# An attention and gated-convolution kernel on one core: sums over 576 columns, 66 weight columns, a 64-row mask, another order of TensorE's runs and shifted due times

## The chip, the cores and the metric

The program runs on one core of one Trainium2 chip. The metric is device time in microseconds of one execution. Five engines take part, each with an instruction queue of its own: TensorE (PE, the matmuls; PEld is its weight load), VectorE (DVE), ScalarE (ACT), GpSimd (POOL) and SyncE (SP), which issues all transfers.

## What is computed

```python
# q, k, v: (8, 8, 576, 64); s: (8, 8, 576)
scores = q @ k.T / sqrt(64)
cum = cumsum(maximum(s, 0))
scores = where(causal, -1e9, scores + minimum(cum_k - cum_q, 0))
attn = exp(scores - max(scores)); attn = attn / (sum(attn) + 1e-9)
x = (attn @ v) as (8, 576, 512)
h = maximum(x @ w_in, 0)                       # w_in: 512 x 1024
conv = three taps along the sequence, one weight per channel
out = (h * sigmoid(conv)) @ w_out              # w_out: 1024 x 512
```

## The kernel before

**Pairs.** The 64 heads (8 batches of 8) are worked in 32 pairs; one head of a pair lies in partitions 0 to 63, the other in 64 to 127, so TensorE works both at once in tiles of 64 rows. The sequence of 576 is cut into tiles of 128 (the last has 64). Only the half of the scores that the causal mask keeps is computed: 576, 448, 320, 192 and 64 columns for the five key tiles. A pair has these tasks, named by a prefix and the pair's number:

- `sh` (L803): a first score pass that gives each row's maximum, in four parts of two matmul steps; `mx` (L820, L825): the maxima on VectorE; `tn`, `rt`, `ds`: they are turned, copied and sent into tile `eq`.
- `sc` (L884): the scores proper, keys on partitions, in four parts (288; 288; 448 and 64; 320 and 192 columns) of four steps each, two PSUM banks a part; `ex` (L906): the exponential on ScalarE into `pt`; `mk` (L919): the triangular part is cleared on GpSimd.
- `ad` (L962): the exponentials of tiles 1 (its last 320 columns) to 4 are added into tile `ad`, three additions a head, on VectorE or GpSimd.
- `sum` (L997): column sums by matmul with a one-hot weight, in tiles of 32 weight columns; `pv` (L944): the values, also in 32-column tiles; `gd`, `inv`, `ri`, `rb`, `nm`: the inverse of the sum is spread over the partitions by way of DRAM, and the values are multiplied by it; `xh`, `xl` split the result in two parts for the next stage.
- `hi` (L756) and `lo` (L760) split queries and keys in two parts before the pair's scores; `dr` (L770) loads the rows of the bias into `ek`.

The second stage works a batch, once its four pairs are done, in two halves: `h` (L1094, 8 blocks of 12 matmuls), ScalarE and VectorE work on each, `ul` (L1161) on GpSimd, then `o` (L1189, 4 blocks of 24 matmuls), `oe` and `st`.

**Early and late pairs.** For pairs before `B0 = 9` the causal mask is added to the scores on TensorE by matmuls of `mask` and `unit` with all 128 rows (L888), there is no `ad`, and the sums go over all 1600 columns. From pair 9 on, `mk` and `ad` are used and TensorE's work is bound in groups: group n holds the `sh` of pair n+1, the `sc` of pair n and the `sum` and `pv` of pair n-1, in the order of the table `ORDER`, and nothing else runs on TensorE in between. The first of a group waits for all that its members need.

```python
ORDER = ("sh0", "sh1", "sh2", "sum", "pv", "sc0", "sh3", "sc1", "sc2", "sc3")
```

**The order of the rest.** A planner (`Sched.play`) runs the task graph once with estimated durations and gives each engine, whenever it is free, the ready task with the smallest due time (`tag`). The order that comes out is the program order of each engine's queue; on the chip only semaphores hold it. The planner also picks PSUM banks and buffers, lets an addition go to VectorE or GpSimd, and does not let operations that are marked as needing both engines' shared way to memory run on both at once.

Of the kernel before, what the change touches and what calls it, by code (L numbers as in the profile page):

```python
# [59 lines left out]
ORDER = ("sh0", "sh1", "sh2", "sum", "pv", "sc0", "sh3", "sc1", "sc2", "sc3")  # L60

# [240 lines left out]
def kernel(  # L302
# [44 lines left out]
    unit = const.tile([P, P], BF16, name="unit")  # L347
# [3 lines left out]
    junk = const.tile([P, S], BF16, name="junk")  # L351
# [16 lines left out]
    ad_t = const.tile([P, 2, W_T[2]], F32, name="ad")  # L368
# [3 lines left out]
    ri_t = const.tile([P, RS], F32, name="ri")  # L372
# [88 lines left out]
    def c_ident(e):  # L461
        make_identity(nc, ident)
        nc.gpsimd.tensor_copy(unit, ident)
# [258 lines left out]
    direct = []  # L722
    last_ek, last_v, last_nm = [None], [None], []
# [8 lines left out]
    def c_rt(n):  # L732

        return n * 0.461e-3

    def pair(p):
# [30 lines left out]
        def d_rows(e):  # L767
# [9 lines left out]
            [last_ek[0], *t_pads[: p + 1]] + (t_bx if 2 * p < DIRECT else [t_rows_d]), a_sh - DRA, d_rows,  # L777
# [9 lines left out]
        for i, part in enumerate(SH_PARTS):  # L787
            pbs = [psb(), psb()]

            def sh_mm(e, part=part, pbs=pbs):  # L790
                o = 0
                for tau, c0, c1 in part:
                    dst = [bank(pb, o, o + c1 - c0) for pb in pbs]
                    qs = slice(P * tau, P * tau + P)
                    for k in range(2):
                        for j, r in enumerate(lanes):
# [10 lines left out]
            t_mm = add(f"sh{p}.{i}", [("PE", 2 * c_rt(w))], [t_hi, t_dr, t_eb],  # L807
# [4 lines left out]
            for j in range(2):  # L812
                o = 0
                for tau, c0, c1 in part:
                    def sh_max(e, j=j, tau=tau, c0=c0, c1=c1, o=o, pb=pbs[j]):
# [17 lines left out]
                        add(f"mx{p}.{j}.{tau}.{c0}", [("DVE", (0.15 if tau == L and c0 == 0 else 0.22) + (c1 - c0) / 0.96e3)],  # L833
# [31 lines left out]
        for i, part in enumerate(SC_PARTS):  # L865
            pbs = [psb(), psb()]

            def sc_mm(e, part=part, pbs=pbs):
                o = 0
                for t, c0, c1 in part:  # L870
                    i0, cn = P * t + c0, c1 - c0
                    ks = slice(P * t, P * t + P)
                    dst = [bank(pb, o, o + cn) for pb in pbs]
                    st = S_t[sb.slot].rearrange("p a c -> p (a c)")
                    for k in range(4):
                        for j, r in enumerate(lanes):
                            if k < 3:
                                kk, kq = ((2, 3), (0, 3), (2, 1))[k]
                                l = st[r, kk * S + P * t : kk * S + P * t + P]
                                m = st[r, kq * S + i0 : kq * S + i0 + cn]  # L880
                            else:
                                l = EK_t[ek.slot][r, ks]
# [417 lines left out]
```

## Time and profile before

| what | value |
|---|---|
| device time, three runs | 810.75, 812.44 and 814.55 us (median 812.44) |
| span of the profiled execution, first to last instruction | 810.0 us |
| TensorE busy | 772.9 us (95%) |
| VectorE busy | 596.5 us (74%) |
| ScalarE busy | 442.1 us (55%) |
| GpSimd busy | 311.6 us (38%) |
| chain that ended last, TensorE's share | 87% |

The device time of the profiled execution itself is not listed apart from its span; the timed runs lie 0.75 to 4.55 us above the span. A busy share is a mean over stages that have different limits; matmuls overlap, so a busy TensorE need not be one at its peak. What a change is worth is read in the stage where it acts.

### The profile page before, as it was taken

How to read it: one execution, taken by the hardware profiler on the slowest of the kernel's cores; microseconds unless marked ns; L12 is line 12 of the kernel's file. 1: busy time of each engine (PE TensorE's matmuls, PEld its weight loads, DVE VectorE, ACT ScalarE, POOL GpSimd, SP SyncE). 2: the span in 40 equal slices, each digit the busy share in tenths (PEclk: the TensorE clock that was granted, in tenths of full speed). 3: DMA queues.
4: the chain of work that ended last, by engine and by line, in shares of the span. 5: the costliest groups of instructions: out<-in, count | busy, mean ns of one | idle time of the engine just before them, and what ended most of it. 6: DMA issues, size and time to landing. Idle time of an engine off the chain costs nothing.

```text
span 810.0 us, 21043 instructions
## 1 busy us (share of the span) xinstructions
PE 772.9 (95%) x8371; PEld 693.5 (86%) x8371; DVE 596.5 (74%) x1379; ACT 442.1 (55%) x982; POOL 311.6 (38%) x411
## 2 busy tenths in 40 slices
PE   2699998989999999999999999999999999999998
PEld 2576777779998999999998999999998999998997
DVE  8779778885577778777778778777777778734632
ACT  4364565637455645646555645646455645645633
POOL 7054452433334443443434443543434433422212
PEclk9999999999999999999999999999999999999999
DMA  7355433320213222122213222132213211111001
GB/s 221 122 161 153 134 100 95 120 89 19 82 46 87 77 82 75 46 90 74 82 45 91 73 82 75 46 92 72 83 45 92 72 54 44 44 42 41 16 23 37
DMA packets 49805, 63.24 MB, mean 78 GB/s; under 512 B 5679, under 2 KB 38767, under 8 KB 49647
## 3 DMA queue, kind: packets, MB, share of 16 engines
q1 hardware_dynamic: 49707, 61.91, 25.1%
q8 instruction: 65, 1.06, 0.5%
q14 instruction: 33, 0.27, 0.1%
HBM read 48.60 MB, written 13.04 MB: 76 GB/s over the span
## 4 chain that ended last, share of the span: by engine, by line
PE 87%; DVE 4%; ACT 2%; POOL 2%; DMA 2%; issue 2%; SPq 0%; ACTq 0%; DVEq 0%; POOLq 0%
PE ps L1189 25%; PE ps L1094 25%; PE ps L884 15%; PE pv L944 10%; PE ps L803 6%; PE ps L997 5%; ACT pt L906 1%; DMA ek<-bx 1%; DVE junk L825 1%; DVE ct L1131 1%; PE ps L888 1%; DMA rb<-ri_d 1%; DVE ct L612 0%; ACT s L756 0%; DVE ct L1119 0%
## 5 line engine op out<-in xcount | busy, mean ns | idle before, releaser
L1189 PE MATMUL ps<-u,wo 128*128 128x288 f32 x1536 | 218.0, 299 | 2.0 <-POOL u L1161 1.4
L1161 POOL TENSOR_TENSOR u<-ct,u 128x576 fp32r<-128x576 f32 x64 | 96.7, 1510 | 314.2 <-ACT u L1157 286.2
L1094 PE MATMUL ps<-x,wi 128*128 128x290 f32 x1536 | 215.9, 298 | 0.0
L1189 PEld LDWEIGHTS ps<-u,wo 128*128 128x128 f32 x1536 | 207.6, 188 | 4.7 <-POOL u L1161 1.9
L1094 PEld LDWEIGHTS ps<-x,wi 128*128 128x128 f32 x1536 | 209.1, 190 | 1.1
L906 ACT ACTIVATE pt<-ps,bias_sb 128x288 f32<-128x288 f32 (+4 forms) x384 | 153.5, 477 | 64.7 <-PE ps L884 64.3
L1131 DVE SCALAR_TENSOR_TENSOR ct<-ht,cw_sb,ct 128x288 f32<-128x288 f32 (+1 forms) x256 | 134.3, 525 | 71.7 <-ACT ct L1117 66.8
L825 DVE CUSTOM_DVE_ANT_0 junk<-ps,mask 128x448 bf16<-128x448 f32 (+3 forms) x256 | 108.3, 423 | 27.7 <-PE ps L803 3.5
L884 PE MATMUL ps<-s 64*128 64x288 f32 (+4 forms) x1152 | 125.1, 314 | 3.3 <-DVE r L825 2.5
L884 PEld LDWEIGHTS ps<-s 64*128 64x128 f32 x1152 | 101.7, 189 | 13.0 <-ACT pt L906 5.7
L1105 ACT ACTIVATE ht<-ps 128x289 f32<-128x289 f32 x128 | 52.7, 412 | 83.6 <-PE ps L1094 82.1
L944 PE MATMUL pv<-pt,v 128*32 128x448 f32 (+4 forms) x1536 | 96.0, 395 | 0.0
L919 POOL TENSOR_SCALAR_AFFINE_SELECT pt<-pt 128x128 f32<-128x128 f32 x230 | 67.3, 312 | 73.2 <-ACT pt L906 70.8
L760 POOL TENSOR_TENSOR s<-raw,s 128x1152 fp32r<-128x1152 f32 x31 | 86.5, 2790 | 15.3 <-ACT s L756 9.6
L944 PEld LDWEIGHTS pv<-pt,v 128*32 128x32 f32 x1536 | 54.9, 111 | 38.0 <-issue 29.8
L884 PE MATMUL ps<-eq,ek 64*128 64x288 f32 (+4 forms) x384 | 74.4, 325 | 0.0
L803 PE MATMUL ps<-s 64*128 64x288 f32 (+4 forms) x384 | 66.5, 331 | 6.0 <-DVE r L820 3.2
L1117 ACT ACTIVATE ct<-ht,cw_sb 128x288 f32<-128x288 f32 x126 | 67.7, 537 | 5.8
L1206 ACT COPY ob<-ps 128x288 f32<-128x288 f32 x63 | 25.0, 397 | 80.5 <-PE ps L1189 68.1
L1150 DVE TENSOR_TENSOR ct<-ct,ht 128x576 f32<-128x576 f32 x64 | 54.4, 851 | 16.7 <-ACT ct L1144 16.7
L803 PE MATMUL ps<-ek,eb 64*128 64x288 f32 (+4 forms) x384 | 58.2, 320 | 6.4 <-DMA ek<-bx 6.4
L1144 ACT ACTIVATE ct<-ct 128x576 f32<-128x576 f32 x64 | 43.6, 681 | 31.5 <-DVE ct L1131 31.2
(87 smaller groups left out, 802.8 us busy)
## 6 DMA issues: line engine op xcount, KB each, us to landing
raw<-qk SPq DMA_DIRECT2D x32, 576.0 KB
v<-vp SPq DMA_DIRECT2D x32, 320.0 KB
rb<-ri_d SPq DMA_DIRECT2D x64, 144.0 KB
outT<-ob SPq DMA_DIRECT2D x64, 144.0 KB
ht<-w_out SPq DMA_DIRECT2D x16, 256.0 KB
w<-w_in SPq DMA_DIRECT2D x8, 512.0 KB
ri_d<-ri SPq DMA_DIRECT2D x32, 72.0 KB
rows_d<-bx SPq DMA_DIRECT2D x1, 1215.0 KB
```

Of the source, the lines that this page charges most:

```text
L760: tt_on(e)(st[:, 0:2, :], R_t[raw.slot], st[:, 2:4, :].bitcast(F32), op=ALU.subtract)
L803: nc.tensor.matmul(dst[j], l, m, start=(k == 0), stop=(k == 1))
L825: nc.vector.tensor_tensor_reduce(out=junk[:, 0 : c1 - c0], in0=bank(pb, o, o + c1 - c0), in1=mask[:, S - w + c0 : S - w + c1], scale=1.0, ...
L884: nc.tensor.matmul(dst[j], l, m, start=(k == 0), stop=(k == 3))
L906: nc.scalar.activation(PT_t[pts[j].slot][0:jt, O_T[t] + c0 : O_T[t] + c1], bank(pb, o, o + c1 - c0)[0:jt], AF.Sigmoid, bias=bias_sb[0:jt, ...
L919: nc.gpsimd.affine_select(out=reg, in_=reg, pattern=[[1, dg]], compare_op=ALU.is_ge, fill=0.0, base=0, channel_multiplier=-1,)
L944: nc.tensor.matmul(pvt[gs, o0 : o0 + c1 - c0], vt[0:jt, t, gs], PT_t[pts[g // 2].slot][0:jt, O_T[t] + c0 : O_T[t] + c1], start=(t == 0), s ...
L1094: nc.tensor.matmul(bank(hb, 0, XW), l, r, start=(k == 0), stop=(k == len(seq) - 1))
L1117: nc.scalar.activation(o, src, AF.Copy, scale=w)
L1131: nc.vector.scalar_tensor_tensor(cc[:, lo:hi], h_[:, sh + lo : sh + hi], cw_sb[:, 3 * f + k : 3 * f + k + 1], cc[:, lo:hi], op0=ALU.mult, ...
L1161: tt_on(e)(uu[:, 1], C_t[ct.slot], uu[:, 0].bitcast(F32), op=ALU.subtract)
L1189: nc.tensor.matmul(bank(pb, 0, HS), l, r, start=(fp == 0 and k == 0), stop=(fp == NF // 2 - 1 and k == len(seq) - 1),)
```

## The change

There are seven parts.

1. `ORDER` is now sums, values, then score parts and maxima parts in turn.
2. For late pairs `ad` has a fourth addition, over 448 columns, so that it covers tiles 0 (from column 128) to 4. The sums then go over 128 columns of `pt` and 448 of `ad`: 576 a head in place of 1024. One head is finished before the other.
3. The score matmuls of the last key tile load 66 weight columns in place of 128.
4. The early mask is built on 64 rows (`mrow`, which lies in the memory of `ad`, and `unit` of 64 columns) and is added in steps of 64 columns, inside the 64-row tiles. It is also added in `sh`, so that the early maxima are plain reductions. Late additions wait for the last use of `mrow`.
5. The planner's price of score and maxima parts has a floor for narrow matmuls.
6. A table `DUE` shifts the due time of nearly every task by its own number; the code that adds it stands at the end.
7. `ri` is no tile of its own any more (the reciprocal is made in place), `junk` is smaller, and the second `dr` no longer waits for the first.

```diff
-ORDER = ("sh0", "sh1", "sh2", "sum", "pv", "sc0", "sh3", "sc1", "sc2", "sc3")
+ORDER = ("sum", "pv", "sc0", "sh0", "sc1", "sh1", "sc2", "sh2", "sc3", "sh3")
...
+DUE = {
...
+        "0 10.83 1 6.21 2 3.03 3 -14.83 4 -47.29 5 82.43 6 30.85 7 -2.83 8 5.75 9 -54.34 "
...
+        nc.gpsimd.memset(mrow, 0.0)
+        for j in range(2):
+            for i in range(2):
+                h = mrow[D * j : D * j + D, 0, i]
+                nc.gpsimd.affine_select(
...
-            [last_ek[0], *t_pads[: p + 1]] + (t_bx if 2 * p < DIRECT else [t_rows_d]), a_sh - DRA, d_rows,
+            [last_ek[0] if p > 1 else None, *t_pads[: p + 1]] + (t_bx if 2 * p < DIRECT else [t_rows_d]), a_sh - DRA, d_rows,
...
+                        if k and p < B0 and tau < L:
+                            for i_ in range(0 if tau else 1, 2):
+                                for j, r in enumerate(lanes):
+                                    d0 = c1 - c0 - D * (2 - i_)
+                                    nc.tensor.matmul(
+                                        dst[j][:, d0 : d0 + D], mrow[r, 1, i_], unit[r],
+                                        start=False, stop=False,
+                                    )
...
-                        if tau == L and c0 == 0:
+                        if plain(tau, c0):
...
+                    kn = min(P, J_T[t] + 2)
+                    dst = [bank(pb, o, o + cn)[0:kn] for pb in pbs]
...
-                                l = st[r, kk * S + P * t : kk * S + P * t + P]
+                                l = st[r, kk * S + P * t : kk * S + P * t + kn]
...
-                            for j in range(2):
-                                nc.tensor.matmul(
-                                    dst[j][:, 0:dg], mask[:, S - P : S], unit[:, 0:dg],
-                                    start=False, stop=False,
-                                )
+                            for i_ in range(dg // D):
+                                for j, r in enumerate(lanes):
+                                    nc.tensor.matmul(
+                                        dst[j][:, D * i_ : D * i_ + D], mrow[r, 0, i_, 0:kn], unit[r],
+                                        start=False, stop=False,
+                                    )
...
-                for t in range(2, NT):
+                for t in range(1, NT):
...
-                        (0, pt[:, 0:S]), (P, pt[:, O_T[1] : O_T[1] + P]), (2 * P, ad_t[:, j, :])
+                        (0, pt[:, 0:P]), (P, ad_t[:, j, :])
...
-            nc.vector.reciprocal(ri_t, rs_t)
+            nc.vector.reciprocal(rs_t, rs_t)
...
+    for t in sch.tasks:
+        t.tag += shift.get(due(t.name), 0.0)
```

How many matmuls of `h` and `o` stand between two groups also changes: between the sums of pairs 9 to 31 there were 60, 72, 120 or 132 of them, and now there are 48 in nine of the places, 72 in two, and 96 to 168 elsewhere.

TensorE at the sums of a late pair, before (`pt_92`, `pt_93`: the two heads' exponentials; the first row is the end of the maxima part `sh2`, the last one the start of the values):

```order
L803 MATMUL ps_70<-ek_84,eb 128x64
L997 MATMUL ps_65<-pt_92,onehot 32x144 x4
L997 MATMUL ps_65<-pt_93,onehot 32x144 x4
L997 MATMUL ps_65<-pt_92,onehot 32x16
L997 MATMUL ps_65<-pt_92,onehot 32x112
L997 MATMUL ps_65<-pt_93,onehot 32x16
L997 MATMUL ps_65<-pt_93,onehot 32x112
L997 MATMUL ps_65<-ad,onehot 32x32
L997 MATMUL ps_65<-ad,onehot 32x144 x2
L944 MATMUL pv<-pt_92,v_91 32x128 x2
```

The same place now, where L1328 is `o` and L1136 and L1082 are the sums and values:

```order
L1328 MATMUL ps_65<-u_1188,wo 128x288 x6
L1136 MATMUL ps_66<-pt_92,onehot 32x128
L1136 MATMUL ps_66<-ad,onehot 32x16
L1136 MATMUL ps_66<-ad,onehot 32x144 x3
L1136 MATMUL ps_66<-pt_93,onehot 32x128
L1136 MATMUL ps_66<-ad,onehot 32x16
L1136 MATMUL ps_66<-ad,onehot 32x144 x3
L1082 MATMUL pv<-pt_92,v_90 32x128 x2
```

The sums have 10 matmuls in place of 18 and follow the `o` matmuls directly; the maxima parts have moved behind the score parts.

GpSimd between two groups that stand close together, before (L919 is `mk`, L962 `ad`, L760 `lo` of the next pair, L1161 `ul`; the first row is the fifth clearing of this pair):

```order
L919 AFFINE_SELECT pt_93<-pt_93 128x128
L919 AFFINE_SELECT pt_93<-pt_93 64x64
L919 AFFINE_SELECT pt_92<-pt_92 128x128 x2
L919 AFFINE_SELECT pt_93<-pt_93 128x128 x2
L962 TENSOR_TENSOR ad<-ad,pt_92 128x192
L962 TENSOR_TENSOR ad<-pt_93 128x320
L760 TENSOR_TENSOR s_83<-raw_81,s_83 128x1152
L1161 TENSOR_TENSOR u_977<-ct_107,u_977 128x576
```

And now, with 48 matmuls between the groups (L1057 is `mk`, L1099 `ad`, L883 `lo`):

```order
L1057 AFFINE_SELECT pt_93<-pt_93 128x128
L1057 AFFINE_SELECT pt_93<-pt_93 64x64
L1099 TENSOR_TENSOR ad<-pt_92 128x448
L1057 AFFINE_SELECT pt_92<-pt_92 128x128
L1099 TENSOR_TENSOR ad<-pt_93 128x448
L1057 AFFINE_SELECT pt_92<-pt_92 128x128
L1057 AFFINE_SELECT pt_93<-pt_93 128x128 x2
L883 TENSOR_TENSOR s_82<-raw_80,s_82 128x1152
```

Both wide additions stand between the clearings, and the other six go to VectorE. In all, 42 of the 46 wide additions are GpSimd's.

SyncE at the start, before (`ek_84` and `ek_85` belong to pairs 0 and 1):

```order
L770 DMA ek_84<-bx 9x1x576 x2
L544 DMA rows_d<-bx 60x5184
L744 DMA raw_81<-qk 128x1152
L770 DMA ek_85<-bx 9x1x576 x2
L770 DMA ek_86<-rows_d 9x576 x2
```

And now:

```order
L893 DMA ek_84<-bx 9x1x576 x2
L893 DMA ek_85<-bx 9x1x576 x2
L665 DMA rows_d<-bx 60x5184
L867 DMA raw_81<-qk 128x1152
L893 DMA ek_86<-rows_d 9x576 x2
```

The load for pair 1 has moved ahead of the store of `rows_d` and of the load of `raw_81`.

## Rows read from the trace of the kernel before

**Rows 1.** The page: its first line.

```profile
span 810.0 us, 21043 instructions
```

**Rows 2.** Busy time in stretches: from, to, length; PE, PEld, DVE, ACT, POOL; clock; DMA.

```profile
41.00:211.00 170.00, 160.51 (x1859) 130.51 (x1860) 134.28 (x334) 94.72 (x222) 69.23 (x47) 0.97 0.36 108
211.00:702.00 491.00, 490.47 (x5511) 450.09 (x5513) 382.39 (x882) 277.10 (x623) 202.34 (x303) 1.00 0.23 70
```

**Rows 3.** Timeline of PE, one group: start us, length us, line, operation, shape, count.

```profile
347.56 0.40 PE L803 MATMUL ps<-s 64*128 64x288 f32 x2
347.79 0.30 PE L803 MATMUL ps<-ek,eb 64*128 64x288 f32 x2
347.92 0.30 PE L803 MATMUL ps<-s 64*128 64x288 f32 x2
...
348.65 0.28 PE L803 MATMUL ps<-ek,eb 64*128 64x64 f32 x2
348.86 0.79 PE L997 MATMUL ps<-pt,onehot 128*32 128x144 f32 x22
...
349.82 0.30 PE L944 MATMUL pv<-pt,v 128*32 128x128 f32 x1
...
352.67 0.68 PE L884 MATMUL ps<-s 64*128 64x288 f32 x6
...
355.43 0.44 PE L884 MATMUL ps<-s 64*128 64x64 f32 x5
...
355.93 0.68 PE L884 MATMUL ps<-s 64*128 64x320 f32 x5
...
357.12 1.06 PE L1189 MATMUL ps<-u,wo 128*128 128x288 f32 x6
```

**Rows 4.** Timeline of PE at two changes of tile shape.

```profile
347.33 0.29 PE L1189 MATMUL ps<-u,wo 128*128 128x288 f32 x1
...
711.09 0.29 PE L1189 MATMUL ps<-u,wo 128*128 128x288 f32 x1
711.31 0.33 PE L997 MATMUL ps<-pt,onehot 128*32 128x144 f32 x4
```

**Rows 5.** Chain that ended last: start, length, line, count.

```profile
368.74 1.60 PE ps L1189 x12
```

**Rows 6.** Weight loads by form: count, busy us, mean ns of one, idle before.

```profile
L884 PEld LDWEIGHTS ps<-s 64*128 64x128 f32 x1152 | 101.7, 189 | 13.0 <-ACT pt L906 5.7 <-DVE r L825 3.6 <-issue 0.5
L944 PEld LDWEIGHTS pv<-pt,v 128*32 128x32 f32 x1536 | 54.9, 111 | 38.0 <-issue 29.8
```

**Rows 7.** Timeline of ACT, the same group.

```profile
353.56 0.89 ACT L906 ACTIVATE pt<-ps,bias_sb 128x288 f32<-128x288 f32 x2 [1.73 <-PE ps L884]
...
356.08 2.99 ACT L906 ACTIVATE pt<-ps,bias_sb 128x448 f32<-128x448 f32 x8 [0.37 <-PE ps L884]
```

**Rows 8.** Tile `ad`: additions on VectorE (ns min/median/max), on GpSimd (busy us, mean ns).

```profile
L962 DVE TENSOR_TENSOR ad<-ad,pt x69: 210/346/2877, 224.0 to 724.3; 128x64 f32<-128x64 f32 x46, 128x192 f32<-128x192 f32 x23
...
L962 POOL TENSOR_TENSOR ad<-pt 128x320 f32<-128x320 f32 x5 | 4.4, 888 | 0.0
```

**Rows 9.** Timeline of GpSimd: one `lo`.

```profile
342.66 2.89 POOL L760 TENSOR_TENSOR s<-raw,s 128x1152 fp32r<-128x1152 f32 x1 [0.46 <-ACT s L756]
```

**Rows 10.** Timelines of SyncE, GpSimd and TensorE at the start.

```profile
14.19 0.48 SPq L544 DMA_DIRECT2D rows_d<-bx  x1
...
16.48 4.22 SPq L770 DMA_DIRECT2D ek<-bx  x2
...
11.95 1.40 POOL L486 MEMSET ek<- 10x576 f32 x2
...
24.58 0.75 PE L803 MATMUL ps<-ek,eb 64*128 64x288 f32 x2 [5.11 <-DMA ek<-bx]
```

**Rows 11.** Maxima on VectorE by form, 20 to 210 us.

```profile
L825 DVE CUSTOM_DVE_ANT_0 junk<-ps,mask 128x448 bf16<-128x448 f32 x19 | 11.8, 622 | 3.5 <-PE ps L803 1.3 <-DVE r L825 0.7 <-ACT wo L688 0.2
L825 DVE DVE_READ_ACCUMULATOR2_ANT r<- 128x1 f32 x96 | 8.0, 83 | 0.0
```

More of the change, by code (lines that the diff above doesn't have):

```diff
@@ L59, with due @@
 B0 = 9
-ORDER = ("sh0", "sh1", "sh2", "sum", "pv", "sc0", "sh3", "sc1", "sc2", "sc3")
+ORDER = ("sum", "pv", "sc0", "sh0", "sc1", "sh1", "sc2", "sh2", "sc3", "sh3")
+KINDS = {
+    "sh": ("mx",), "tn": ("rt", "ds"), "sc": ("ex", "mk", "ad"), "pv": ("sum",),
+    "nm": ("gd", "inv", "ri", "rb", "xh", "xl"), "g": ("re", "ce", "ta", "ga", "mu", "uh", "ul"),
+    "o": ("oe", "st"),
+}
+DUE = {
+    "x":
+        "s -33.34 masks -20.61 ident 7.58 eb -10.97 cum 15.92 rows_d -2.56 bias_cp 15.79 cw 4.06 "
+        "cwq 18.7 cwh 29.2",
+    "pads":
+        "0 4.99 1 20.21 2 -5.6",
+    "ind":
[78 rows of a table added]
+}
+def due(name):
+    kind, rest = re.match(r"([a-z]+)(.*)", name).groups()
+    if not rest or kind in ("bias", "rows"):
+        return "x:" + name
+    for of, kinds in KINDS.items():
+        if kind in kinds:
+            kind = of
+    n = 2 if kind in ("h", "g", "o", "wo") else 1
+    return kind + ":" + ".".join(re.findall(r"^[\d.]*", rest)[0].split(".")[:n])
 class Buf:
@@ L350 @@
     cw_sb = const.tile([P, NF * 3], F32, name="cw_sb")
-    junk = const.tile([P, S], BF16, name="junk")
+    junk = const.tile([P, W_T[1]], BF16, name="junk")
     wi = const.tile([P, 2, NC, DF], F32R, name="wi")
@@ L366 @@
     rb_t = const.tile([P, S], F32, name="rb")
-    ad_t = const.tile([P, 2, W_T[2]], F32, name="ad")
+    ad_t = const.tile([P, 2, W_T[1]], F32, name="ad")
+    mrow = ad_t.bitcast(BF16).rearrange("p a c -> p (a c)")[:, 0 : 4 * P].rearrange(
+        "p (k i m) -> p k i m", k=2, i=2
+    )
     R8_t = [const.tile([P, P], F32, name=f"r{i}") for i in range(2)]
@@ L462, in c_ident @@
         make_identity(nc, ident)
-        nc.gpsimd.tensor_copy(unit, ident)
+        nc.gpsimd.tensor_tensor(unit, ident[:, 0:D], ident[:, D:P], op=ALU.add)
+        nc.gpsimd.memset(mrow, 0.0)
[3 more added lines that the diff above has]
+                nc.gpsimd.affine_select(
+                    out=h, in_=h, pattern=[[-1, P]], compare_op=ALU.is_ge, fill=NEG,
+                    base=D * i, channel_multiplier=1,
+                )
+                h = mrow[D * j : D * j + D, 1, i]
+                nc.gpsimd.affine_select(
+                    out=h, in_=h, pattern=[[1, P]], compare_op=ALU.is_ge, fill=NEG,
+                    base=-D * i, channel_multiplier=-1,
+                )
         nc.gpsimd.memset(mask, 0.0)
@@ L730, with c_rt @@
                 [(2, 0, W_T[2]), (3, 0, W_T[3])]]
-    def c_rt(n):
-        return n * 0.461e-3
+    def c_rt(part, last=P):
+        return sum(max((c1 - c0) / 2.4e3 + 0.013, 0.107 if t < L else last / 1.2e3)
+                   for t, c0, c1 in part)
     def pair(p):
@@ L806, in pair @@
             w = sum(c1 - c0 for _, c0, c1 in part)
-            t_mm = add(f"sh{p}.{i}", [("PE", 2 * c_rt(w))], [t_hi, t_dr, t_eb],
+            t_mm = add(f"sh{p}.{i}", [("PE", 2 * c_rt([(0, *x[1:]) for x in part]) + (0 if p >= B0 else 0.06 * sum(2 if tau else 1 for tau, _, _ in part if tau < L)))],
+                       [t_hi, t_dr, t_eb, t_ident],
                        a_sh + 0.1 * i, sh_mm, alloc=pbs + ([r8] if i == 0 else []),
@@ L986, in sums @@
             n = len(rows[0])
[L987 to L1002 removed]
+            steps = [(i, j) for i in range(n) for j in range(2)]
+            if ad:
+                steps = [(i, j) for j in range(2) for i in range(n)]
+            for i, j in steps:
+                c0, src = rows[j][i]
+                c1 = c0 + src.shape[1]
+                for q in range(c0 // RS, 4):
+                    g = 3 - q if j else q
+                    a_, b_ = max(c0, q * RS), min(c1, (q + 1) * RS)
+                    if a_ >= b_:
+                        continue
+                    o0 = a_ - q * RS
+                    nc.tensor.matmul(
+                        bank(sb_, o0, o0 + b_ - a_)[32 * g : 32 * g + 32], onehot[:, j, :],
+                        src[:, a_ - c0 : b_ - c0], start=j == 0 and (i == 0 or (ad is not None and q > 0)),
+                        stop=j == 1 if ad else i == n - 1, tile_position=(0, 32 * g),
+                        skip_group_check=True,
+                    )
         ta = A1 + 1
         tq = ta - TQA
[L1006 removed]
+        t_sum = add(f"sum{p}", [("PE", 0.6 if ad else 1.4)], [t_ident] + added + [m for t, m in masks[0] + masks[1]], tq, sums,
                     alloc=[sb_], uses=[*pts] + ([ad] if ad else []), mode="c32", burst=group(p + 1))
```

51 lines of the change are left out of this document (21 added, 30 removed), and 77 rows, old and new, of the table DUE.

## The prediction

> **What bounds the kernel now.** The busy time in stretches comes first [rows 2]: from 211 to 702 us, where the groups run, TensorE is busy 490.5 of 491 us at the full 2.4 GHz (clock 1.00), VectorE 78%, ScalarE 56%, GpSimd 41%. From 41 to 211 us TensorE is busy 160.5 of 170 us and VectorE 134.3 (79%); there waits hide inside matmul rows that overlap, so I don't call it TensorE-bound. The timeline of one group shows what can be saved [rows 3]: the maxima parts start at 347.56, the sums at 348.86, the values at 349.82, the scores at 352.67, and `o` is back at 357.12: 9.56 us, 23 times. In the middle stretch a microsecond off TensorE's run is a microsecond off the time, if nothing that TensorE waits for comes later.
>
> **Sums.** They take 0.96 us (348.86 to 349.82 [rows 3]). Each of the four 32-column tiles gets a share: by the row listing the fullest got 144+112+32 columns of one head and 288 of the other, 576, so 1.67 ns a column. Now each gets 144 a head, 288: 0.48 us. That is 0.48 us less for 23 pairs: **11.0 us**. Bounds: nothing, if the start of a run of such matmuls is what costs (18 rows become 10), and 11.0.
>
> **66 weight columns.** Eight score matmuls of 64 columns take 0.50 us (355.43 to 355.93 [rows 3]): four steps of both heads, 0.125 each, though 64 columns at the pace of the 288-column steps (0.13 us, 347.79 to 347.92) would need 0.03. So the weight load sets the pace. A load of 128 columns lasts 189 ns, one of 32 111 ns [rows 6]: 0.81 ns a column, 50 ns for 62 columns. Four steps: 0.20 us, 23 late pairs: **4.6 us**. Lower bound nothing, upper four times 0.09 us (down to the pace of the columns), 8.3. In early pairs I count nothing: there the scores wait for ScalarE, whose 16 exponentials take 5.5 us a pair (353.56 to 359.07 [rows 7]).
>
> **One change of tile shape less.** A group went from full tiles to 64-row, to 32-column, to 64-row, to full tiles; now the second step falls out. Going into 64-row tiles costs 0.10 us at the start (347.33 to 347.56 [rows 3, 4] against 0.133 us for an `o` matmul [rows 5]) and 0.10 on the next step (0.23 against 0.13 [rows 3]); from 64-row to 32-column tiles the last step takes 0.21 us (348.65 to 348.86) against 0.125: 0.09. What comes in, full to 32-column, stands at 711.09 to 711.31 [rows 4]: 0.22 against 0.133, 0.09. Net 0.20 us, 23 times: **4.6 us**; bounds 2 and 6.
>
> **Score and maxima parts in turn.** Six banks, two a part. Scores are emptied by ScalarE (5.5 us a pair [rows 7]), maxima by VectorE (622 plus 83 ns for 448 columns [rows 11], in proportion some 5 us for a pair's 3200). Before, three maxima parts drained under the values; one score part still waited some 0.3 us for a bank (the idle 0.37 between exponentials [rows 7] is the other side of this). Now both streams are fed over some 4.5 us of TensorE time and each is longer than that, so the last parts wait for the exponential and maximum two parts earlier. Following the banks by these durations, I get 0.1 before the third score part and 0.25 before the last maxima part. I take no difference; bounds 0.3 us either way, 7 us over 23 groups.
>
> **The wide additions.** GpSimd takes 888 ns for 320 columns [rows 8], so an estimate for 448, in proportion, is 1.24 us; 42 such come on. Its load of 41% [rows 2] allows that, and in gaps of 72 and more matmuls (9.6 us and more at 0.133 [rows 5]) they lie under `h` and `o`. In the nine gaps of 48 (6.4 us) they may not. Counted from the start of the scores, the exponentials end at 6.4 us (352.67 to 359.07 [rows 3, 7]). With both wide additions among the clearings, the last clearing ends between 6.8 and 9.3 us. A last head's additions of 320, 192 and 64 columns take at most 0.89 and about 0.35 and 0.21 us [rows 8]: the sums could start at 8.2 to 10.7. TensorE comes at 5.3 + 6.4 + 0.2 = 11.9. So they are hidden, unless `lo` gets between: one lasts 2.89 us [rows 9], and additions of 64 and 192 columns, 210 ns at the least, reached 2877 [rows 8]: they were held for a whole `lo`. Then the sums start at up to 13.6 us and TensorE waits 1.7; I take 1.3, since VectorE gets some of the additions in first. The clearing order puts `lo` right behind the last clearing, where the additions are due, so it gets between in about half of the cases: 0.7 us in each of the nine, **6 us lost**; bounds nothing and, with a second block by `ul`, 2.8 us each, 25.
>
> The Trainium skill (SBUF — State Buffer, Who interferes with whom) says that VectorE with two inputs in SBUF and GpSimd reading SBUF exclude each other for the whole instruction, whichever started first. Rows 8 and 9 agree: the worst addition, 2877 ns, lasts as long as one `lo`. By this rule alone each of the nine gaps would lose a whole `lo` whenever it starts before the last addition, 1.3 us each, 12 us in all, and the sum below would come out 6 us higher.
>
> **The early stage.** Pair 1's maxima waited for its bias rows until 24.58, since their load was issued at 16.48, behind the store of `rows_d` of 14.19 [rows 10]. Now it goes ahead of it. But GpSimd must build `mrow` first: a memset and eight selects. The nearest row is a memset of `ek`, 0.7 us for one of two [rows 10]; at 0.4 to 0.7 each this is 3.5 to 6 us, after which the last fill of `ek` (that ended at 13.35) ends at 17 to 19. With some 3 us for a load that waits for nothing, pair 1 starts at 20 to 22, 2.5 to 4.5 us sooner. The store of `rows_d`, and the weights behind it, come 3 to 5 us later, with 20 us and more before they are needed. VectorE loses 72 reads of the accumulator (83 ns [rows 11]), 6 us of 134, and the mask's matmuls stay in one tile shape, which takes some 0.2 us a pair off but adds 14 small matmuls in the maxima. The shifted due times reorder everything; no row prices them. I take **6 us** in all; bounds a loss of 4 (weights late) and a gain of 16 (4.5 at the start and a third of the 36 us from 41 to 211 us in which VectorE, the busiest there beside TensorE, is idle [rows 2]).
>
> The reciprocal in place, the smaller `junk` and the planner's prices cost nothing by themselves. The end (702 us on) keeps its pattern.
>
> **Sum.** 11.0 + 4.6 + 4.6 + 6 - 6 = 20.2 us off the span of 810.0 [rows 1]: 789.8. The timed runs' median lies 2.4 us above this span; I leave that: **792 us**.
>
> **Rivals.**
> - *The sums wait for the additions.* In favour: the fourth addition, 48 matmuls in place of at least 60, and the sums now first, without 1.3 us of maxima ahead of them [rows 3]. Against: the planner knows of the shared memory, and TensorE did not wait in this stretch before. With 1.3 to 2.5 us in each of nine gaps it loses 12 to 22 in place of 6: 798 to 808. The skill's rule, named above, gives the lower of the two.
> - *The due times do more.* If they close that third of VectorE's early idle time, 10 us beyond my 6: 782, and with no wait at the additions 776.
> - *The gain is not on the path.* If ScalarE's 5.5 us and VectorE's 5 us a pair bind the turn of parts, the weight columns and shape change are given back (9.2) and 0.3 us a group besides: 11.0 for the sums less 6 of waits and 7 of banks leaves nothing but the start: 808, and without that 814.
> - *Slower.* If in all 23 groups the sums wait longer than the 0.88 us that a group saves. In the nine short gaps alone that needs 2.2 us each, with nothing gained early: two blocks, by `lo` and then `ul`, give 2.8, so with the first three terms' 20.2 it is 812.4 - 20.2 + 25 = 817; with weights late by 4 us, 821.
>
> **Chances.** A measurement of this kernel tells about 0.5% (4 us) from no change. My forecast (783 to 798) 0.55; waits at the sums (798 to 808) 0.18; due times (below 783) 0.15; not on the path (808 to 816) 0.07; slower 0.05. Range 778 to 805: it leaves out about 0.05 below and 0.15 above.
>
> **What would show it.** In the profile after: sums of 0.5 us with the values right behind; eight 66-column score matmuls in 0.3 us; no idle of TensorE at the sums (waits for VectorE or GpSimd there mean the first rival); the maxima wait at 24.58 gone by 22; a group of 8.7 us. A group at 9.2 or more means the banks. An idle TensorE after a group, waiting for `ad`, in all nine short gaps would make the prediction wrong upwards; a first group much before 205 us, downwards.

## The result and the profile after

The changed kernel takes 793.25 us (median; 792.84 to 796.83), beside 812.88 us of the kernel before on the same chip: ratio 0.977, 95% interval 0.9741 to 0.9798. The forecast was 792 us. Its profiled execution spans 791.1 us, 18.9 less than before [rows 1].

The page's first line, and the busy time in two stretches of the changed kernel (columns as in [rows 2]):

```profile
span 791.1 us, 20607 instructions
...
41.00:198.00 157.00, 148.87 (x2028) 127.64 (x2030) 131.87 (x280) 89.51 (x214) 66.50 (x47) 0.96 0.37 113
210.00:700.00 490.00, 487.43 (x5174) 444.10 (x5174) 377.33 (x880) 292.61 (x636) 237.19 (x339) 1.00 0.23 70
```

TensorE still fills the middle, but not as fully as before: 2.6 us of idle in 490, where [rows 2] had 0.5 in 491. The early stage ends about 13 us sooner: the group with pair 8's sums starts at 197.5 us, where it started at 210.8. The total came out as forecast, its parts did not. The table shows this. It adds up TensorE's time by kind of matmul, each counted from its start to the start of the next (so waits count with the matmul ahead of them; the turns `tn` are counted with `o`), from pair 9's first sums (column "from") to the start of the last matmul ("to"), in one profiled execution of every kernel of this study (the letters are the experiments below):

```
kernel                    from      to    sums  values  scores,maxima      h      o   total
before                   240.1   805.8    22.5    65.3          123.0   168.3   186.5   565.7
changed                  227.2   787.0    20.0    65.7          120.1   166.5   187.6   559.8
a 128 columns            227.4   790.4    19.8    65.7          123.6   166.3   187.6   563.0
b old sums               228.0   790.1    22.9    65.5          119.9   166.0   187.8   562.2
c one addition           225.4   776.5    13.1    64.5          119.8   166.2   187.6   551.1
d lo after additions     225.8   779.2    13.1    64.5          121.0   166.3   188.5   553.4
e no DUE                 228.4   787.9    13.1    64.5          124.1   172.0   185.8   559.5
f old mask               261.0   822.0    20.4    65.9          124.8   166.6   183.2   561.0
g short maxima           225.7   782.4    20.9    65.7          116.1   167.7   186.4   556.7
h additions and start    225.0   778.4    13.1    64.5          121.1   166.3   188.4   553.4
i before, new mask       235.1   800.9    22.5    65.3          123.0   168.3   186.7   565.8
j old score mask         235.6   795.5    20.0    65.7          120.2   166.5   187.6   559.9
k old maxima             226.3   786.3    20.1    65.7          120.1   166.5   187.7   560.0
l old order, no DUE      229.5   806.8    14.0    71.2          137.1   170.0   185.1   577.3
```

Where the late work is the same (changed, j, k) the totals agree within 0.2 us. The starts are less steady: those of the kernels that do the same early work in the same order (changed, a, b, c, d, g) lie between 225.4 and 228.0.

Two things must be put right before the first two lines are compared. In the kernel before, 1.3 us of maxima stand ahead of the sums ([rows 3]: 347.56 to 348.86), and the changed kernel has made 12 matmuls of `h` more (1.6 us) by its first sums. At equal work the stretch went from 567.0 to 561.4 us, 5.6 less, and what lies ahead of it lost 13.2 (238.8 to 225.6). The forecast had 14.2 and 6.

One group of the changed kernel, in a gap where nothing waits, TensorE (start, length, line, tiles, count; L1136 sums, L1082 values, L1019 scores, L934 maxima, L1328 `o`):

```profile
406.80 0.30 PE L1136 MATMUL ps<-pt,onehot 128*32 128x128 f32 x1
...
407.37 2.87 PE L1082 MATMUL pv<-pt,v 128*32 128x128 f32 x48
410.17 0.66 PE L1019 MATMUL ps<-s 64*128 64x288 f32 x6
...
411.59 0.74 PE L934 MATMUL ps<-s 64*128 64x288 f32 x2
411.94 0.52 PE L934 MATMUL ps<-ek,eb 64*128 64x288 f32 x2
412.18 0.84 PE L1019 MATMUL ps<-s 64*128 64x448 f32 x5
...
413.08 0.28 PE L1019 MATMUL ps<-s 64*66 64x64 f32 x2
...
415.85 0.40 PE L1328 MATMUL ps<-u,wo 128*128 128x288 f32 x1
```

It answers to [rows 3]: 9.05 us where 9.56 stood and 8.7 was forecast. The sums take 0.57 us (407.37 less 406.80), not 0.48. Scores and maxima take 5.68 (410.17 to 415.85), where some 5.3 was forecast; the two maxima steps at 411.59 and 411.94 lie 0.35 us apart, and their like in [rows 3] 0.13: most likely a wait that ends inside overlapping matmuls and gets no idle time of its own (experiment g bears on it).

And a gap of 48 matmuls, at 508 to 516 us: GpSimd (additions, the subtraction for `u` of L1300, and `lo` of L883), VectorE, TensorE:

```profile
508.14 1.16 POOL L1099 TENSOR_TENSOR ad<-pt 128x448 f32<-128x448 f32 x1
509.28 1.43 POOL L1300 TENSOR_TENSOR u<-ct,u 128x576 fp32r<-128x576 f32 x1
510.67 2.66 POOL L883 TENSOR_TENSOR s<-raw,s 128x1152 fp32r<-128x1152 f32 x1
...
508.84 5.57 DVE L1099 TENSOR_TENSOR ad<-ad,pt 128x192 f32<-128x192 f32 x4
514.33 0.76 DVE L1201 TENSOR_TENSOR x<-rb,x 128x580 fp32r<-128x580 f32 x1
...
513.61 0.97 PE L1136 MATMUL ps<-ad,onehot 128*32 128x144 f32 x4 [0.56 <-DVE ad L1099]
...
515.27 0.31 PE L1136 MATMUL ps<-ad,onehot 128*32 128x144 f32 x1 [0.37 <-DVE ad L1099]
```

Four additions take 5.57 us here (five take 1.80 in experiment d). They come free when `lo` ends (513.33), and a last one stands behind the subtraction for `x`; the sums of this gap last 2.69 us. Of the tile `ad`, the additions on VectorE and the wide ones on GpSimd (41 of its 42 lie in this window, 210 to 710 us), as in [rows 8]:

```profile
L1099 DVE TENSOR_TENSOR ad<-ad,pt x117: 208/345/4709, 211.5 to 704.3; 128x64 f32<-128x64 f32 x46, 128x192 f32<-128x192 f32 x41, 128x320 f32<-128x320 f32 x30
L1099 POOL TENSOR_TENSOR ad<-pt x41: 1151/1165/1184, 209.8 to 685.3; 128x448 f32<-128x448 f32 x41
```

A wide addition costs 1.17 us (the estimate was 1.24), and the longest of the narrow ones has grown from 2877 to 4709 ns.

Seven of the nine gaps of 48 matmuls show such a wait; in the other six an addition is held through one `lo`, and lasts 2.8 to 3.2 us. The two gaps without a wait, ahead of the sums of pairs 30 and 31, come when GpSimd has no `lo` left to do. Its last one:

```profile
658.13 2.68 POOL L883 TENSOR_TENSOR s<-raw,s 128x1152 fp32r<-128x1152 f32 x1
```

With the waits the sums of all 23 groups take 20.0 us, without them they would take 23 x 0.57 = 13.1.

### The profile page after: what moved, and what is told of

Its sections match the earlier page's. It is cut to its first block, busy times and chain, and to the rows that moved or that the text cites. A ratio compares the mean times of both kernels' runs of the same rounds, so it can differ in the third digit from the quotient of the medians.

```text
span 791.1 us, 20607 instructions
## 1 busy us (share of the span) xinstructions
PE 752.3 (95%) x8201; PEld 679.3 (86%) x8201; DVE 583.5 (74%) x1315; ACT 448.5 (57%) x984; POOL 349.7 (44%) x456
## 4 chain that ended last, share of the span: by engine, by line
PE 83%; DVE 6%; DMA 4%; issue 2%; POOL 2%; ACT 2%; SPq 1%; POOLq 0%; DVEq 0%; ACTq 0%
PE ps L1233 25%; PE ps L1328 22%; PE ps L1019 13%; PE pv L1082 10%; PE ps L934 8%; PE ps L1136 4%; DVE ad L1099 3%; DMA rows_d<-bx 1%; ACT pt L1044 1%; DMA rb<-ri_d 1%; DMA ri_d<-rs 1%; DMA eq<-rt 1%; DVE junk L960 1%; DVE ct L1270 1%; PE ps L976 1%
## 5 line engine op out<-in xcount | busy, mean ns | idle before, releaser
L1328 PE MATMUL ps<-u,wo 128*128 128x288 f32 x1536 | 220.2, 298 | 2.3 <-POOL u L1300 1.2
L1328 PEld LDWEIGHTS ps<-u,wo 128*128 128x128 f32 x1536 | 207.7, 189 | 5.9 <-POOL u L1300 1.9
L1300 POOL TENSOR_TENSOR u<-ct,u 128x576 fp32r<-128x576 f32 x64 | 95.9, 1498 | 236.4 <-ACT u L1296 215.8
L1270 DVE SCALAR_TENSOR_TENSOR ct<-ht,cw_sb,ct 128x288 f32<-128x288 f32 (+1 forms) x256 | 140.5, 553 | 60.0 <-ACT ct L1256 54.6
L1019 PE MATMUL ps<-s 64*128 64x288 f32 (+4 forms) x1152 | 123.1, 305 | 6.8 <-DVE r L955 6.0
L1019 PEld LDWEIGHTS ps<-s 64*128 64x128 f32 (+1 forms) x1152 | 98.9, 179 | 13.7 <-DVE r L955 6.6
L1057 POOL TENSOR_SCALAR_AFFINE_SELECT pt<-pt 128x128 f32<-128x128 f32 x230 | 59.9, 284 | 106.0 <-ACT pt L1044 98.0
L960 DVE CUSTOM_DVE_ANT_0 junk<-ps,mask 128x64 bf16<-128x64 f32 (+3 forms) x184 | 78.0, 424 | 24.9 <-PE ps L934 11.9
L883 POOL TENSOR_TENSOR s<-raw,s 128x1152 fp32r<-128x1152 f32 x31 | 85.3, 2751 | 22.7 <-DVE s L879 13.0
L1082 PE MATMUL pv<-pt,v 128*32 128x448 f32 (+4 forms) x1536 | 94.3, 390 | 0.0
L1082 PEld LDWEIGHTS pv<-pt,v 128*32 128x32 f32 x1536 | 54.2, 110 | 37.2 <-issue 24.1
L934 PE MATMUL ps<-s 64*128 64x288 f32 (+4 forms) x384 | 78.9, 343 | 7.2 <-DVE r L955 3.7
L955 DVE TENSOR_REDUCE r<-ps 128x1 f32<-128x288 f32 (+4 forms) x136 | 52.1, 430 | 29.3 <-PE ps L934 29.0
L934 PE MATMUL ps<-ek,eb 64*128 64x288 f32 (+4 forms) x384 | 68.8, 333 | 2.6 <-DMA ek<-bx 2.6
L1019 PE MATMUL ps<-eq,ek 64*128 64x288 f32 (+4 forms) x384 | 70.3, 308 | 0.1
L1099 DVE TENSOR_TENSOR ad<-ad,pt 128x192 f32<-128x192 f32 (+2 forms) x117 | 68.1, 625 | 1.1 <-POOL ad L1099 1.0
```

Source lines behind the costliest of these rows:

```text
L883: tt_on(e)(st[:, 0:2, :], R_t[raw.slot], st[:, 2:4, :].bitcast(F32), op=ALU.subtract)
L934: nc.tensor.matmul(dst[j], l, m, start=(k == 0), stop=(k == 1))
L960: nc.vector.tensor_tensor_reduce(out=junk[:, 0 : c1 - c0], in0=bank(pb, o, o + c1 - c0), in1=mask[:, S - w + c0 : S - w + c1], scale=1.0, ...
L1082: nc.tensor.matmul(pvt[gs, o0 : o0 + c1 - c0], vt[0:jt, t, gs], PT_t[pts[g // 2].slot][0:jt, O_T[t] + c0 : O_T[t] + c1], start=(t == 0), s ...
L1099: tt_on(e)(acc, pt[:, P:S] if t == 1 else acc, pt[:, O_T[t] : O_T[t] + W_T[t]], op=ALU.add,)
L1270: nc.vector.scalar_tensor_tensor(cc[:, lo:hi], h_[:, sh + lo : sh + hi], cw_sb[:, 3 * f + k : 3 * f + k + 1], cc[:, lo:hi], op0=ALU.mult, ...
```

## The experiments

All ratios are to the kernel before on the same chip; the change's own is 0.977, and 0.001 is 0.8 us. "List" is the order in which instructions are issued. Unless it says otherwise, an experiment keeps the change's list and alters only what an entry issues.

**a. 128 weight columns.**

```diff
-                    kn = min(P, J_T[t] + 2)
+                    kn = min(P, J_T[t] + 2) if p < B0 else P
```

> The change, but score matmuls of the late pairs load 128 weight columns again (66 before); order and everything else as in the change. If the weight load sets the pace of the 64-column blocks and that pace is on the path, 0.20 us come back in each of 23 groups: +4.6 us, 797.9. If the turn of parts is paced by the banks (ScalarE's exponentials, VectorE's maxima), the 0.2 us hide in the waits for a bank that the change has in a group: +0 to +1, 793 to 794.

796.27 us, 0.9833 (0.9819 to 0.9848): 5 us slower than the change by the ratios, and in the table scores and maxima grow by 3.5 us, 0.15 a group. Weight loads of the scores, by form, from 210 to 700 us of the changed kernel:

```profile
L1019 PEld LDWEIGHTS ps<-s 64*128 64x128 f32 x660 | 57.6, 185 | 2.8
...
L1019 PEld LDWEIGHTS ps<-s 64*66 64x66 f32 x132 | 10.9, 134 | 0.4
```

The load falls by 51 ns for 62 columns (the two rows are different blocks of one kernel); the term of 4.6 us is borne out within the measurement.

**b. The old sums, without the wide additions.**

```diff
-                        (0, pt[:, 0:P]), (P, ad_t[:, j, :])
+                        (0, pt[:, 0:S]), (P, pt[:, O_T[1] : O_T[1] + P]),
+                        (2 * P, ad_t[:, j, P:])
...
+                        if t == 1:
+                            return
```

> The change, but the sums run over 1024 columns as before and the additions of 448 columns are not made; the order of everything else stays. Sums cost 0.40 us more in 23 groups (0.97 against 0.57), +9.2. If the wide additions are what makes the sums late in seven short gaps, those 8 us of waits go with them: 794.5. If it is `lo` on GpSimd that holds VectorE's additions, which are still made, the waits stay: 802.

794.83 us, 0.9816 (0.9799 to 0.9833). The sums take 0.97 us in all groups but one (1.36), so without the wide additions the waits are gone but for that one, of 0.4 us; what the narrow sums and the wide additions are worth together is the difference, 3.7 us by the ratios and 2.4 by the table. They win 23 x 0.40 = 9.2 and give most of it back as waits.

**c. One addition a head.**

```diff
                     def pre_add(e, j=j, t=t):
+                        if t > 1:
+                            return
```

> The change, but of the four additions a head of the late pairs only the first, of 448 columns, is made (part of the sums is left out). If the 8 us that TensorE idles at the sums come from the small additions being held on VectorE, they go: 785.5. If the wide additions or the clearings before them are late by themselves, or something else is late right behind, most stays: 791 to 793.

783.11 us, 0.969 (0.9663 to 0.9717). Sums fall to 13.1, values by 1.2 (the late sums had run into them): 8.1 us of waits, all gone with the narrow additions, which are left out here on both engines. (In the change's seven gaps the addition that `lo` holds is VectorE's.) The wide additions alone, still made, do not delay the sums.

**d. GpSimd's later work behind the additions.** In seven gaps (pairs 10, 14, 16, 18, 20, 22 and 28) the entries of GpSimd between its last clearing or addition and the last addition of all, and the subtraction for `x`, move behind that addition; ahead of them GpSimd gets a small operation that reads the results:

```diff
+            last = ad_t[:, :, W_T[1] - 1 : W_T[1]]
+            nc.gpsimd.tensor_tensor(scr, last, last, op=ALU.add)
```

> The change, but in the seven gaps of 48 matmuls in which TensorE waited, GpSimd's next work (`lo` of a later pair, or the subtraction for `u`) starts only when the last addition is made (a small GpSimd operation reads its result), and the subtraction for `x` stands behind it on VectorE. If `lo` and that subtraction hold VectorE's additions, six to eight of the 8 us go: 786. If the additions are late for their own number, nothing changes (793); if `lo` then comes late for its scores, it gets slower, by up to 2.7 us a gap, 7 x 2.7 = 19.

785.38 us, 0.9711 (0.969 to 0.9731): faster than both kernels. The gap shown above, now (POOL, DVE, PE):

```profile
506.23 0.58 POOL L1396 TENSOR_TENSOR scr<-ad 128x2 f32<-128x2 f32 x1 [1.49 <-DVE ad L1101]
506.77 1.43 POOL L1302 TENSOR_TENSOR u<-ct,u 128x576 fp32r<-128x576 f32 x1
508.16 2.66 POOL L885 TENSOR_TENSOR s<-raw,s 128x1152 fp32r<-128x1152 f32 x1
...
504.29 1.80 DVE L1101 TENSOR_TENSOR ad<-ad,pt 128x192 f32<-128x192 f32 x5
...
508.08 0.30 PE L1138 MATMUL ps<-pt,onehot 128*32 128x128 f32 x1
...
508.65 2.87 PE L1084 MATMUL pv<-pt,v 128*32 128x128 f32 x48
```

Five additions in 1.80 us, sums in 0.57, no wait, and `lo` in time for its scores: GpSimd idles 1.49 us instead. The sums of all groups come to 13.1. This gives back 6.4 of c's 8.7 us in the table without leaving an addition out.

**e. No DUE.** The shifts of the due times are all zero, so the planner makes another list.

```diff
-        t.tag += shift.get(due(t.name), 0.0)
+        t.tag += 0.0
```

> The change without the table DUE (all shifts zero), so the planner's own due times order the work; sums, weight columns, mask and the turn of parts as in the change. The first late group began 13.3 us earlier than in the kernel before, 7 more than was forecast. If the table gave those 7, the group begins at about 205 and the time is 800 (ratio to the kernel before 0.985). If they come from the mask and the maxima, the group begins at 197 to 199 and the time stays within 2 us of the change (0.977).

793.01 us, 0.979 (0.9748 to 0.9832): no difference that can be measured. The group with pair 8's sums starts at 201.6 us, between the two marks of the expectation (the change: 197.5), and pair 9's sums at 228.4, 1.2 later than in the change. From there no sums wait (no gap is as short as 48 matmuls), but `h` takes 5.5 us more (3.2 of them 24 matmuls that came ahead in the change) and scores and maxima 4.0 more. At equal work, then, e is 4.4 us later at pair 9's sums and takes 3.5 us less from there on. The table DUE, the longest piece of the diff, is worth nothing in the total that shows: it wins some 4 us early and gives them back in the groups, and without it the planner makes a list as good.

**f. The old mask,** both halves: in the early scores one matmul of 128 rows, in the early maxima VectorE adds the mask and reads an accumulator.

```diff
-                        if k and p < B0 and tau < L:
+                        if False:
...
-                        return c0 == 0 and (tau == L or p < B0)
+                        return c0 == 0 and tau == L
...
+                                    dst[j][:, 0:dg], mask[:, S - P : S - P + kn], unit2[:, 0:dg],
```

> The change, but the early pairs' mask goes the old way (one matmul of 128 rows in the scores, VectorE's maxima add the mask and read an accumulator), in the change's order. If VectorE's 72 reads of the accumulator (83 ns each, 6 us) and the mask's tile shapes are worth what was forecast, the first late group begins some 6 us later and the time is 799 (0.985); if VectorE's early work has slack, 0 to 2 us, 793 to 795.

823.3 us, 1.0175 (1.0123 to 1.0227): 33 us slower than the change, far beyond either expectation. But this is not the change's list, as the expectation has it. The function `plain`, which the edit alters, also gives the planner its price of an early maximum (0.15 us, or 0.22 where `plain` is false), and with the new prices the planner made another list: ahead of pair 9's sums stand 228 matmuls of `o`, where the change has 192. From those sums on f takes 561.0 us, 1.2 more than the change (the 36 matmuls of `o` that are already done, 4.8 us, help it); all else is lost before. The early stretch, changed kernel and then this one:

```profile
41.00:200.00 159.00, 150.87 (x2084) 129.35 (x2086) 132.13 (x281) 89.86 (x215) 67.91 (x48) 0.96 0.37 115
```

```profile
41.00:200.00 159.00, 144.91 (x1591) 113.10 (x1588) 118.13 (x313) 80.75 (x190) 53.37 (x38) 0.88 0.34 105
```

VectorE, which the old maxima load more, is not full: it is busy less than in the change. TensorE idles 6 us more, and its granted clock is 0.88 where it was 0.96: 0.08 x 159 = 13 us of matmuls at the full clock. That holds for the profiled execution (828.63 us). Two others of this kernel had a mean granted clock of 0.990 over the whole, where the change's profiled one has 0.991, and still took 819.2 and 822.62 us; so the clock is not the main part of the 33 us.

**j, k. Each half by itself, in the change's list:** only the mask of the scores goes the old way (j), only that of the maxima (k). Here the planner's prices stay as they are.

> The change, but the early scores' mask by one matmul of 128 rows again; order, maxima and everything else as in the change. By 0.25 us a block, 45 blocks, +11 us (804.5, ratio to the kernel before 0.991). Both halves of the old mask together gave +33 us (1.0175): if this half is the one that does it, it gives 25 and more (1.008).

> The change, but the early maxima add the mask on VectorE and read an accumulator again (72 reads of 83 ns, 6 us in all), and TensorE adds none; order as in the change. If VectorE's 6 us are on the path, 3 to 6 us (0.981 to 0.984); less the 0.06 us of each small mask matmul, some 5 us of TensorE, it can come out at nothing (0.977). If this half makes the 33 us, 20 and more (1.0).

j: 801.15 us, 0.9871 (0.9839 to 0.9903), 8 us slower, all of it before 235.6 us (the change: 227.2). k: 793.89 us, 0.9806 (0.9771 to 0.9841), not to be told from the change. So the scores' half is the one that counts; the maxima's half, with 72 accumulator reads more on VectorE and the small mask matmuls spared on TensorE, comes out even. 8 and 3 are not 33: some 22 us of f belong to neither half by itself. They stand beside another list, and no run has both halves in the change's list, so f says nothing on whether the halves add up.

**i. The kernel before with the new mask of the scores,** in its own list.

```diff
+                            for i_ in range(dg // D):
+                                for j, r in enumerate(lanes):
+                                    nc.tensor.matmul(
+                                        dst[j][:, D * i_ : D * i_ + D], mrow[r, i_], half[r],
```

> The kernel before, in its own order, with one thing of the change: the mask of the early pairs' scores in 64-row matmuls (and the table for it, built by GpSimd). In the trace of before a mask matmul of 128 rows between 64-row ones costs a score block about 0.25 us more than the blocks of the change take, five blocks a pair, nine pairs: 11 us. If TensorE is the early stage's path, the time falls by that: ratio 0.986. If the early scores wait for ScalarE, as the prediction had it, at most 0.2 us a pair: 0.998 to 1.0.

806.57 us, 0.9949 (0.993 to 0.9969): 4.1 us, pair 9's sums 5.0 us earlier, between the two expectations. Less than half of the 11 us shows in the list of before, 8 of it in that of the change (j). What keeps back the rest in i is not shown; a part can be the clock, whose mean up to pair 9's sums was 0.96 in i and 0.98 in the kernel before (0.02 x 235 = 5 us at the most). Two score blocks with their mask, before and then changed (L888 and L1024 are the masks):

```profile
112.36 0.69 PE L884 MATMUL ps<-s 64*128 64x320 f32 x6
112.98 0.28 PE L888 MATMUL ps<-unit,mask 128*128 128x128 bf16 x2
113.20 0.41 PE L884 MATMUL ps<-eq,ek 64*128 64x320 f32 x2
113.45 0.47 PE L884 MATMUL ps<-s 64*128 64x192 f32 x6
```

```profile
107.35 0.69 PE L1019 MATMUL ps<-s 64*128 64x320 f32 x6
107.88 0.23 PE L1024 MATMUL ps<-unit,ad 64*128 64x64 bf16 x4
107.95 0.39 PE L1019 MATMUL ps<-eq,ek 64*128 64x320 f32 x2
108.17 0.47 PE L1019 MATMUL ps<-s 64*128 64x192 f32 x6
```

1.09 us for a block of 320 columns, and 0.82, both at a granted clock of 1.00: two mask matmuls in 128-row tiles, with the way into them and back, cost 0.27 us more than four in 64-row tiles. Of the nine early pairs, eight have 1.08 to 1.09 us here before, and all have 0.82 to 0.85 in the change. A pair has five blocks with a mask; for the other four widths the cost is not shown. The Trainium skill (TensorEngine Tiling (Array Packing), Key Properties) says that changing the tiling mode drains TensorE; it gives no price, and these rows agree with it.

**g. Short maxima.**

```diff
+                        if p >= B0:
+                            nc.vector.tensor_reduce(
+                                out=acc, in_=bank(pb, o, o + 16),
```

> The change, but each maximum of the late pairs looks at 16 columns only (part of the maxima is left out), so VectorE frees a maxima part's banks at once. If VectorE's maxima are what stretches the turn of parts (5.7 us measured against 5.3), 0.4 us go in each of 23 groups, 9 us, and with VectorE's lighter load some of the 8 us of waits at the sums: 780 to 785. If the parts wait for ScalarE's exponentials, or for the weight loads, the run stays at 5.6 us and the time at 788 to 793.

788.58 us, 0.9745 (0.97 to 0.9789): between the expectations, and by the intervals not clearly apart from the change. In the table scores and maxima lose 4.0 us, 0.17 a group, less than half of the 9 that VectorE was charged with; the waits at the sums stay, as they should, since `lo` still stands where it did.

**h. Additions and start.** Kernel d, with the load of pair 0's shifts (`ds0`) ahead of the loads that wait for the store of `rows_d`, and the split of the first weights behind pair 1's maxima and pair 0's first exponentials:

```diff
+    order = behind("ds0", ("dr2", "wi6", "wi0", "wi2"))
+    order = behind("ex0.0.0.288", ("wi6q", "wi61", "wi0q", "wi01", "wi02", "wi2q", "wo3.0q"))
```

> The kernel of the run before with GpSimd's later work behind the additions (ratio 0.971), and at the start the load of pair 0's shifts goes out ahead of the loads that wait for the store of `rows_d`, and pair 1's maxima and pair 0's first exponentials stand ahead of the split of the first weights on VectorE and ScalarE. If the 5.6 us that TensorE waits for pair 0's scores at 25 us are VectorE standing at those weights, most of it goes: 5 us, ratio 0.965. If another wait ends at the same time (the shifts, the second pair's rows), 0 to 2 us: 0.969 to 0.971.

785.34 us, 0.9705 (0.9658 to 0.9753): the same as d. The start of the changed kernel (PE, SP, DVE), and then of this one (PE, DVE):

```profile
19.89 0.73 PE L934 MATMUL ps<-s 64*128 64x288 f32 x2
...
26.29 1.50 SPq L727 DMA_DIRECT2D w<-w_in  x3
...
29.79 0.43 DVE L733 TENSOR_SCALAR w<-w 128x512 uint32<-128x512 uint32 x1 [5.53 <-DMA w<-w_in]
...
30.93 0.60 PE L1019 MATMUL ps<-s 64*128 64x288 f32 x1 [5.58 <-DVE r L955]
```

```profile
25.87 1.58 PE L1021 MATMUL ps<-s 64*128 64x288 f32 x6
...
38.99 0.61 PE L936 MATMUL ps<-s 64*128 64x288 f32 x2 [5.70 <-DVE s L881]
...
32.95 0.43 DVE L735 TENSOR_SCALAR w<-w 128x512 uint32<-128x512 uint32 x1 [1.02 <-DMA w<-w_in]
...
37.02 1.82 DVE L881 CAST s<-raw 128x1152 fp32r<-128x1152 f32 x1
```

The scores do start 5.06 us sooner. Then pair 2's maxima wait 5.70 us for a copy that stands behind the same weights on VectorE. The wait was moved, not removed.

**l. The old order of a group, without DUE.**

```diff
-ORDER = ("sum", "pv", "sc0", "sh0", "sc1", "sh1", "sc2", "sh2", "sc3", "sh3")
+ORDER = ("sh0", "sh1", "sh2", "sum", "pv", "sc0", "sh3", "sc1", "sc2", "sc3")
```

> The change without the table DUE (ratio 0.979) and with the old run of a pair: three maxima parts, sums, values, first scores, last maxima, scores. By the prediction's terms one change of tile shape comes back in 23 groups and nothing else: +4.6 us, 0.985. If the turn of parts costs 0.4 us a group in waits for banks that the old run does not have, these 9 us go and it comes out 4 to 5 us faster: 0.973. If the two cancel, 0.978 to 0.980.

811.83 us, 1.0012 (0.9989 to 1.0034): both expectations fell; it is 18 us slower than e, and the table puts all of it into the groups: 13.0 in scores and maxima, 6.7 in the values. Of TensorE's waits, the longest row (us in total, times, longest); one of its five waits, of which four are of this length; and the stretch behind it:

```profile
PE ps L1136 <- DVE r L955: 11.2, 5, 2.7
```

```profile
366.58 0.27 PE L1136 MATMUL ps<-pt,onehot 128*32 128x128 f32 x1 [2.68 <-DVE r L955]
...
367.16 4.57 PE L1082 MATMUL pv<-pt,v 128*32 128x128 f32 x48
```

```profile
366.60:372.00 5.40, 5.40 (x72) 2.61 (x74) 4.29 (x15) 1.16 (x3) 3.47 (x3) 0.68 0.17 35
```

With three maxima parts ahead of them, the sums wait 2.68 us for a bank that VectorE's late maxima hold, and after that the granted clock is 0.68 for 5.4 us, and the values take 4.5 in place of 2.8 (3.6 to 5.3 behind the other three). The run of before had no such wait in its own list: this holds for a list that the planner makes with the new costs, not for the old run as such.

## Why the prediction came out right, and where its parts did not

That the total was right to 1 us is luck: two errors cancel. The middle gained 8.6 us less than forecast, the early stage 7 more. Term by term, forecast and measured in us:

| Term | Forecast | Measured | From |
|---|---|---|---|
| Sums | -11.0 | -9.2 | 0.57 us beside 0.97, 23 times |
| 66 columns | -4.6 | -3.5 | a |
| Change of shape, and the turn of parts | -4.6 and 0 | -0.7 | the rest of the 4.2 that scores and maxima lost at equal work (nothing, if the 66 columns take the 5 us of a's ratio) |
| Waits at the sums | +6 | +8.1 | c |
| Early stage | -6 | -13.2 | table |

**Sums.** The mechanism held, and the price per column was taken as the old one (1.67 ns); it is 0.57/288 = 1.98 ns. **66 columns.** Right in mechanism and, within the measurement, in size; the upper bound of 8.3 was not reached.

**Shape and turn.** Their sum is 4 us short. g shows 4.0 us of waits for VectorE's banks in the turn, inside the 7 us bound that the prediction gave; the value taken, no difference, was the mis-sized one. If the shape change gives back the forecast 4.6 us, the two come to 0.6, about the measured 0.7. That the shape change is worth 4.6 was not shown by itself: l was to show it and was overtaken by another wait.

**Waits at the sums.** The mechanism was the forecast one, a block by `lo`. Its price was right, 1.2 us each on the mean (8.1 over 7) in place of 1.3; its share was not: it came in seven of the nine gaps, which are all that still had a `lo`, where about half was forecast. The gap at 512.60 had the second block, by `u`, that the bound had priced at 2.8. b, c and d agree: the waits need the wide additions ahead of `lo` (b), the narrow additions (c) and `lo` right behind (d). The Trainium skill (SBUF — State Buffer, Who interferes with whom) gave 12 us, since each of nine gaps was to lose a whole `lo`; the trace has 8.1, and for the seven gaps with a `lo` the same price gives 9.1, nearer than the forecast's 6. For one addition its rule is too mild: the one at 508.84 in the changed kernel was held through three GpSimd instructions, 4.7 us, not only for the one that was running.

**Early stage.** This step failed in size, and the term that was too small is the one on the mask: "the mask's matmuls stay in one tile shape, which takes some 0.2 us a pair off". It is 0.27 us a block of 320 columns; if the other widths cost the same, five blocks a pair and nine pairs make 12 us, of which j shows 8. The prediction took it that the early scores wait for ScalarE; i and j show that TensorE's time counts there too. The due times, which it did not price, win some 4 us here (e) and give them back later. What it did count is not to be found: the accumulator reads (k: even) and pair 1's earlier bias rows. The wait for those at 24.58 [rows 10] is gone as forecast (pair 1's maxima start at 19.89), and a wait of 5.58 us at 30.93 came in its place: VectorE stands 5.53 us at weights whose load goes out behind the store of `rows_d`. The prediction had "20 us and more before they are needed". h shows that removing this wait moves it again. 8 and 4 are near the 13.2, but each was measured by itself, and no run shows that they add up.

**The rivals.** Waits at the sums came as a part of the forecast and stayed near its size; the due times do nothing in the total; "not on the path" is refuted by a and by the sums; the slower case needed 2.2 us in each gap, and 0.9 in each of nine was lost.

## What to carry to other kernels

Matmuls of another tile shape inside a run of small ones can cost more than small ones in their place (0.27 us a block here): count the places, not the runs. Where a long GpSimd operation that is due later holds VectorE's short additions that are due now, make it wait for them (d: 6.4 us by the table, 5 by the ratios, for seven 2-column operations). And a wait at the start that an order ends comes back at the next instruction behind the same late load (h): look at what stands behind it before pricing the gain. In a kernel whose order is planned, look whether an edit also reaches the planner's prices: f was to change the mask alone and changed the list with it.

## What was not expected of the hardware

TensorE's granted clock after a wait: behind 2.68 us of idle it was 0.68 for the next 5.4 us (l), below the upper of the two levels (2.4 GHz) for part of that; behind the idle of 0.56 and 0.37 us at 513.61 and 515.27 in the changed kernel it stayed at 1.00, and the values took 3.05 (515.29 to 518.34), beside the last of the sums. VectorE's addition at 508.84 was not let in between GpSimd's instructions: three in a row held it for 4.7 us. The other way seems to hold too: GpSimd's operation on 2 columns took 0.58 us in all seven places (506.23 in d), nearly as long as GpSimd takes for an addition of 192 columns in the changed kernel (0.60), and ended within 0.06 us of VectorE's subtraction for `x` beside it.
